# Row maxima of masked scores: key columns taken 512 and 256 at a time instead of 384 and 384

## The chip, the cores and the metric

The kernel runs on one core of a Trainium2 chip. The metric is the device time of one execution in microseconds (us). Before the change it is 643.86 us, the median of three runs (643.77 to 643.98).

## The reference

Two stages follow each other. The first is attention within clusters, for 4 batches of 8 heads, 768 tokens and 64 values per head:

```
q_assign = argmax over 16 centroids of cosine(q, centroid);  k_assign likewise
scores   = q k^T / sqrt(64), set to -1e9 where q_assign != k_assign
attn     = exp(scores - max(scores)) / (sum + 1e-9);   out = attn v
```

The second treats the 3072 rows of 512 values as tokens: a token is computed if its product with `w_skip` is positive, a gate of 8 experts picks one for it, and `relu(x w1) w2`, times the gate, is added to its row.

## The kernel before

Heads are worked on in pairs, i = 0 to 15; half a of a pair is one head. For a pair the kernel does the following.

**Operands.** q and k are split into a rounded part and a rest (`split_hi`, `split_lo`), the cluster of each token is found on VectorE (`assign`, `first_max`), and one-hot rows of the clusters are set under q and k (`masks`), so that one product of 96 rows gives the rounded score plus the mask.

**Maxima (`smax`, lines 577 to 587).** A product of 128 queries (tile j of 6) with 384 keys (half hf of 2) goes to a PSUM tile of 128x384, and VectorE reduces it to one column of `M`. For 6 tiles, 2 heads and 2 halves these are 24 products (line 582) and 24 reductions (line 584) a pair, 384 of each in all. `mneg` (line 598) then takes the larger of a tile's entries, and `mrows` (line 606) turns them and puts them as six more rows under q, so that a score product has the maximum subtracted.

**Scores (`score`).** For each of 24 (half, key tile, head) two products of 384 columns accumulate in one bank (lines 631, 632), ScalarE takes the exponential (line 634), and GpSimd adds up the sums (lines 640, 646). `avs` (line 657) multiplies the exponentials with v in groups of 12 records, into a bank of its own.

**Order.** Nothing is scheduled at run time. `steps` and `tasks` give every task a due time in steps (one score is one step, 24 to a pair; the numbers are in `PLAN` and, for the first pairs, in `FIRST`), and tasks are written out in that order; each engine then works its own queue in order. Maxima of pair i are due about 21 steps ahead of its first score, one a step, in two series of 12 with a small gap; so PE gets maxima of one pair between the scores of another. The routing of tokens to experts (`route_c`, `route_d` with line 996, and others) is put in between at the end of every fourth pair.

**Banks.** Eight PSUM banks of 128x512 stand as tiles. Bank 7 is kept for `avs` and for filler products; the other seven go round in a queue: `take` gives out the bank that was returned longest ago, and `give`, written right after the instruction that reads the bank, returns it. So with these calls the eighth tile uses the bank of the first, and PE waits at it until the reader of the first is done:

```
b = self.held[key] = self.free.popleft()
self.free.append(self.held.pop(key))
```

**Lead-in.** For pair 0 all of this has to happen before the first score. After each of the first 12 maxima products a filler product of 384 columns is written (`keep_busy`, line 280, `WARM`).

After the pairs come the experts (`experts`): products of 256 columns (`ph`) and 512 columns (`py`) in lines 1056 to 1058, with weights split by ScalarE and VectorE, rows gathered and scattered by indirect DMA.

Of the kernel before, what the change touches and what calls it, by code (L numbers as in the profile page):

```python
# [19 lines left out]
ALU = mybir.AluOpType  # L20
AX = mybir.AxisListType
PSUM = bass.MemoryType.PSUM

P = 128
H, S, D, NCL = 8, 768, 64, 16
HP = H // 2
HALF = S // 2
NB = HALF // P
KT = S // P
# [12 lines left out]
OT = 32  # L42
OC = P // OT
RING = 8
WARM = (0, 12, 3)


PLAN = {
# [33 lines left out]
class Kernel:  # L82
# [243 lines left out]
    def tasks(self, i):  # L326

        p, last = {**PLAN, **FIRST.get(i, {})}, i == self.npair - 1
        r = [(s, lambda s=s: self.score(i, s)) for s in range(NS)]
        add = lambda t, f, *a: r.append((t, lambda: f(i, *a)))  # L330
        if i:
            add(p["load"], self.load)
        add(p["load_v"], self.load_v)
        if i == 2:
            for a in range(2):
                add(8.0 + 6.0 * a - i * NS, self.set_rows, a)
        add(p["sims"], self.sims)
        add(p["assign"][0], self.assign, *p["assign"][1:])
        if i:
            for t in range(2):  # L340
                add(p["hi"][t], self.split_hi, t)
                add(p["lo"][t], self.split_lo, t)
            add(p["copies"][0], self.copies_hi)
            for t in range(2):
                add(p["copies"][1 + t], self.copies_lo, t)
            add(p["masks"][0], self.masks, *p["masks"][1:])
        else:
            for n in range(4):
                add(p["hi"][n], self.hi_first, n % 2, n // 2)
                add(p["lo"][n], self.lo_first, n % 2, n // 2)  # L350
            add(p["masks"], self.masks_first)
        t0, dt, gap, dt2 = (*p["smax"], p["smax"][1])[:4]
        for n in range(24):
            add(t0 + dt * n if n < 12 else t0 + 12 * dt + gap + dt2 * (n - 12), self.smax, n)
        for hf in range(2):
            add(p["mneg"][hf], self.mneg, hf)
            add(p["mrows"][hf][0], self.mrows, hf, *p["mrows"][hf][1:])
            for g in range(0, KT, GROUP):
                add(12 * hf + 2 * (g + GROUP) + p["av"], self.avs, hf, range(g, g + GROUP))
        if not last:  # L360
            add(p["sums"], self.sums, (0, 1))
            add(p["recip"], self.recip)
            for hf in range(2):
                add(p["xout"][2 if hf and i == self.npair - 2 else hf], self.xout, hf)
        if i == self.npair - HP - 1:
            for t, f in zip(p["early"], (self.early_lists, self.early_rows)):
                add(t, f)
        if last:
            for t, f, *a in self.ending(i):
                add(t, f, *a)  # L370
        elif i % HP == HP - 1:
            add(p["route"][0], self.route_a, i // HP)
            add(p["route"][1], self.route_gates, i // HP)
            add(p["route"][2], self.route_slots, i // HP)
        return r
# [199 lines left out]
                self.give((t, hf))  # L575

    def smax(self, i, n):
        c, nc = self.st[i], self.nc
        a, j, hf = n // KT % 2, n // (2 * KT) * NB + n // 2 % NB, n % 2
        c["m"] = self.M[i % 2]  # L580
        sm = self.take("sm", [P, HALF])
        nc.tensor.matmul(sm, lhsT=c["qm"][a][0:96, j * P:(j + 1) * P],  # L582
                         rhs=c["kb"][a][0:96, hf * HALF:(hf + 1) * HALF], start=True, stop=True)
        nc.vector.tensor_reduce(out=c["m"][:, j, a, hf:hf + 1], in_=sm, axis=AX.X, op=ALU.max)  # L584
        self.give("sm")
        if i == 0 and n in range(*WARM[:2]):
            self.keep_busy(1, WARM[2])

# [935 lines left out]
```

## Time and profile before

| | |
|---|---|
| runs | 643.77, 643.86, 643.98 us |
| profiled execution | 643.63 us; span 641.9 us from its first to its last instruction |
| VectorE (DVE) | 506.0 us busy (79%), 1047 instructions |
| ScalarE (ACT) | 425.9 us busy (66%) |
| GpSimd (POOL) | 364.0 us busy (57%) |
| line 584, reductions | 384 instructions |
| line 582, maxima products | 384 instructions, 356 ns each as recorded |

The profile is of one execution. PE is TensorE's products, PEld its weight loads. A product's record lasts longer than its share of the engine, since the next starts while it drains: what a product costs is the distance from its start to the next start. In a timeline the columns are start, duration (of a merged row: from first start to last end), engine, line, operation, tiles, shapes and count, and in brackets the idle time before with what ended it.

### The profile page before, as it was taken

How to read it: one execution, taken by the hardware profiler on the slowest of the kernel's cores; microseconds unless marked ns; L12 is line 12 of the kernel's file. 1: busy time of each engine (PE TensorE's matmuls, PEld its weight loads, DVE VectorE, ACT ScalarE, POOL GpSimd, SP SyncE). 2: the span in 40 equal slices, each digit the busy share in tenths (PEclk: the TensorE clock that was granted, in tenths of full speed). 3: DMA queues.
4: the chain of work that ended last, by engine and by line, in shares of the span. 5: the costliest groups of instructions: out<-in, count | busy, mean ns of one | idle time of the engine just before them, and what ended most of it. 6: DMA issues, size and time to landing. Idle time of an engine off the chain costs nothing.

```text
span 641.9 us, 12202 instructions
## 1 busy us (share of the span) xinstructions
PE 621.7 (97%) x3873; PEld 459.2 (72%) x3873; DVE 506.0 (79%) x1047; ACT 425.9 (66%) x963; POOL 364.0 (57%) x384
## 2 busy tenths in 40 slices
PE   7899999999999999999999999999999999999994
PEld 3566776676667766666767676646799899899793
DVE  6898787699998869999879997885889765855721
ACT  7377788788778877877878878833644644645510
POOL 8697887867867967778777778522043212121101
PEclk9999999999999999999999999999999999999998
DMA  7397748866786466555754652332395766765610
GB/s 215 92 228 204 189 125 210 228 205 176 206 231 179 129 172 168 170 140 162 206 151 124 174 135 75 99 117 86 117 312 196 255 222 223 240 206 177 240 44 36
DMA packets 54322, 110.10 MB, mean 172 GB/s; under 512 B 8599, under 2 KB 22807, under 8 KB 54256
## 3 DMA queue, kind: packets, MB, share of 16 engines
q1 hardware_dynamic: 51232, 101.92, 54.7%
q0 software_dynamic: 2624, 7.18, 3.3%
q8 instruction: 32, 0.52, 0.3%
q14 instruction: 34, 0.28, 0.2%
q10 hardware_dynamic: 400, 0.20, 0.1%
HBM read 60.93 MB, written 10.55 MB: 111 GB/s over the span
## 4 chain that ended last, share of the span: by engine, by line
PE 72%; DMA 10%; issue 9%; DVE 7%; ACT 1%; POOL 0%; POOLq 0%; DVEq 0%; ACTq 0%
PE ps L657 20%; PE ps L631 11%; PE ps L582 11%; PE ps L632 10%; DMA out<-yo,idw 7%; DMA xg<-out,idr 2%; PE ps L488 2%; DVE M L584 2%; PE ph L1058 2%; PE ph L1057 2%; PE ph L1056 2%; PE ps L693 2%; PE ps L756 2%; PE py L1057 1%; PE py L1056 1%
## 5 line engine op out<-in xcount | busy, mean ns | idle before, releaser
L646 POOL TENSOR_TENSOR acc<-acc,PT 128x384 f32<-128x384 f32 x246 | 244.0, 1020 | 42.2 <-ACT PT L634 41.9
L634 ACT ACTIVATE PT<-ps 128x384 f32<-128x384 f32 x384 | 183.2, 492 | 74.2 <-PE ps L632 62.1
L584 DVE TENSOR_REDUCE M<-ps 128x1 f32<-128x384 f32 x384 | 198.5, 550 | 40.3 <-PE ps L582 40.0
L657 PE MATMUL ps<-PT,vt 128*64 128x385 f32 x768 | 138.4, 495 | 0.1
L631 PE MATMUL ps<-D 102*128 102x384 f32 x384 | 134.9, 351 | 2.3 <-DVE M L584 1.7
L582 PE MATMUL ps<-D 96*128 96x384 f32 x384 | 134.4, 356 | 1.0 <-ACT D L562 1.0
L632 PE MATMUL ps<-D 128*128 128x384 f32 x384 | 130.0, 339 | 0.0
L657 PEld LDWEIGHTS ps<-PT,vt 128*64 128x64 f32 x768 | 49.3, 136 | 59.9 <-issue 55.3
L631 PEld LDWEIGHTS ps<-D 102*128 102x128 f32 x384 | 72.8, 190 | 23.8 <-issue 18.6
L582 PEld LDWEIGHTS ps<-D 96*128 96x128 f32 x384 | 73.5, 192 | 21.0 <-issue 14.4
L640 POOL TENSOR_TENSOR acc<-PT 128x384 f32<-128x384 f32 x64 | 54.5, 870 | 58.4 <-ACT PT L634 37.1
L1214 POOL DMA_INDIRECT out<-yo,idw x15 | 20.0, 1335 | 112.6 <-DVE yo L1090 95.3
L632 PEld LDWEIGHTS ps<-D 128*128 128x128 f32 x384 | 73.0, 190 | 0.0
L1342 ACT ACTIVATE hh<-ph 128x256 fp32r<-128x256 f32 x56 | 21.4, 383 | 46.4 <-PE ph L1058 46.4
L1343 DVE SCALAR_TENSOR_TENSOR hl<-ph,hh 128x256 fp32r<-128x256 f32 x56 | 23.6, 422 | 33.6 <-ACT hh L1342 33.6
L1314 ACT ACTIVATE D<-wraw 128x1024 fp32r<-128x1024 f32 (+1 forms) x45 | 44.2, 1002 | 6.5 <-PE py L1058 4.7
L1056 PE MATMUL ph<-x2l,D 128*128 128x256 f32 x168 | 47.7, 284 | 0.0
L1057 PE MATMUL ph<-x2h,D 128*128 128x256 f32 x168 | 47.5, 283 | 0.0
L1056 PE MATMUL py<-D,hh 128*128 128x512 f32 x112 | 45.0, 402 | 0.0
L1315 DVE TENSOR_TENSOR D<-wraw,D 128x1024 fp32r<-128x1024 f32 (+1 forms) x29 | 34.3, 1183 | 6.3 <-ACT D L1314 5.6
L778 ACT ACTIVATE x<-ps,rs 128x64 f32<-128x64 f32 x162 | 36.1, 322 | 3.5 <-issue 1.2
L439 DVE TENSOR_TENSOR raw<-raw,D 128x768 fp32r<-128x768 f32 x28 | 38.2, 1363 | 0.0
(314 smaller groups left out, 1050.5 us busy)
## 6 DMA issues: line engine op xcount, KB each, us to landing
wraw<-w SPq DMA_DIRECT2D x72, 512.0 KB, 4.7
D<-D SPq DMA_DIRECT2D x124, 192.0 KB, 3.4
raw<-qk SPq DMA_DIRECT2D x16, 768.0 KB, 5.5
D<-raw SPq DMA_DIRECT2D x60, 192.0 KB, 4.2
vt<-v SPq DMA_DIRECT2D x16, 384.0 KB, 4.6
out<-x SPq DMA_DIRECT2D x31, 192.0 KB, 3.6
D<-mk SPq DMA_DIRECT2D x120, 24.0 KB, 2.0
out<-yo,idw POOLq DMA_INDIRECT x15, 4.3
```

Of the source, the lines that this page charges most:

```text
L439: eng.tensor_tensor(out=lo.bitcast(F32R), in0=lo, in1=c[f"hi{t}"].bitcast(F32), op=ALU.subtract)
L582: nc.tensor.matmul(sm, lhsT=c["qm"][a][0:96, j * P:(j + 1) * P], rhs=c["kb"][a][0:96, hf * HALF:(hf + 1) * HALF], start=True, stop=True)
L584: nc.vector.tensor_reduce(out=c["m"][:, j, a, hf:hf + 1], in_=sm, axis=AX.X, op=ALU.max)
L631: nc.tensor.matmul(ps, lhsT=c["kb"][a][:MR, ks], rhs=c["qm"][a][:MR, sl], start=True, stop=False)
L632: nc.tensor.matmul(ps, lhsT=c["kc"][a][:, ks], rhs=c["qc"][a][:, sl], start=False, stop=True)
L634: nc.scalar.activation(out=pt, in_=ps, func=AF.Exp, scale=D ** -0.5)
L640: nc.gpsimd.tensor_tensor(out=acc, in0=self.pt(i, s - 2)[:, :HALF], in1=pt, op=ALU.add)
L646: (nc.vector if dve else nc.gpsimd).tensor_tensor(out=acc, in0=acc, in1=pt, op=ALU.add)
L657: nc.tensor.matmul(av[a * D:(a + 1) * D, :], lhsT=c["vt"][:, kt, a * D:(a + 1) * D], rhs=self.pt(i, hf * 2 * KT + kt * 2 + a), start=(kt = ...
L1056: mm(ps, lhsT=ah, rhs=bl, start=first, stop=False)
L1057: mm(ps, lhsT=ah, rhs=bh, start=False, stop=False)
L1314: nc.scalar.activation(out=h[:, cs], in_=r[:, cs], func=AF.Copy)
```

## The change

Four 384-column products of two neighbouring (head, query tile) units become four products into three banks: 512 keys of the first unit, then 256 keys of the first and 256 of the second side by side, then 512 keys of the second. Each bank has one reduction; the middle one reduces 128x2x256 to two columns. A pair has 18 calls in place of 24, due every 4/3 of the former distance. The units of a half are (head 0: tiles 0, 1), (head 0 tile 2, head 1 tile 2), (head 1: tiles 0, 1). In the lead-in 9 filler products of 512 columns replace 12 of 384.

```
-WARM = (0, 12, 3)
+WARM = (0, 9, 4)
...
-        for n in range(24):
-            add(t0 + dt * n if n < 12 else t0 + 12 * dt + gap + dt2 * (n - 12), self.smax, n)
+        for n in range(18):
+            add(t0 + dt * n * 4 / 3 if n < 9 else t0 + 12 * dt + gap + dt2 * (n - 9) * 4 / 3, self.smax, n)
...
-        a, j, hf = n // KT % 2, n // (2 * KT) * NB + n // 2 % NB, n % 2
         c["m"] = self.M[i % 2]
-        sm = self.take("sm", [P, HALF])
-        nc.tensor.matmul(sm, lhsT=c["qm"][a][0:96, j * P:(j + 1) * P],
-                         rhs=c["kb"][a][0:96, hf * HALF:(hf + 1) * HALF], start=True, stop=True)
-        nc.vector.tensor_reduce(out=c["m"][:, j, a, hf:hf + 1], in_=sm, axis=AX.X, op=ALU.max)
+        m = c["m"].rearrange("p j a h -> p (j a h)")
+        j0, (two, part) = n // 9 * NB, divmod(n % 9, 3)
+        ends = (((0, 0), (0, 1)), ((0, 2), (1, 2)), ((1, 0), (1, 1)))[two]
+        at = [((j0 + j) * 2 + a) * 3 for a, j in ends]
+        sm = self.take("sm", [P, 512])
+        parts = ((0, 0, 512),) if part == 0 else ((1, 256, S),) if part == 2 else ((0, 512, S), (1, 0, 256))
+        n0 = 0
+        for u, k0, k1 in parts:
+            a, j = ends[u]
+            nc.tensor.matmul(sm[:, n0:n0 + k1 - k0], lhsT=c["qm"][a][0:96, (j0 + j) * P:(j0 + j + 1) * P],
+                             rhs=c["kb"][a][0:96, k0:k1], start=True, stop=True)
+            n0 += k1 - k0
+        if part == 1:
+            out, sm = m[:, at[0] + 1:at[1] + 1:at[1] - at[0] - 1], sm.rearrange("p (u k) -> p u k", u=2)
+        else:
+            out = m[:, at[0]:at[0] + 1] if part == 0 else m[:, at[1] + 1:at[1] + 2]
+        nc.vector.tensor_reduce(out=out, in_=sm, axis=AX.X, op=ALU.max)
         self.give("sm")
```

## Rows read from the trace of the kernel before

**Rows 1.** Page, busy time: engine, busy us, share of the span, instructions.

```profile
PE 621.7 (97%) x3873; PEld 459.2 (72%) x3873; DVE 506.0 (79%) x1047; ACT 425.9 (66%) x963; POOL 364.0 (57%) x384
```

**Rows 2.** Stretches: from:to, length; busy us of PE, PEld, DVE, ACT, POOL; clock, DMA.

```profile
175.00:189.00 14.00, 12.97 (x88) 8.74 (x86) 13.62 (x30) 10.01 (x29) 9.59 (x11) 1.00 0.84 213
189.00:250.00 61.00, 61.00 (x370) 42.37 (x371) 50.91 (x100) 48.89 (x120) 45.88 (x48) 1.00 0.61 168
```

**Rows 3.** Waits of PE: who waited for whom, us in total, times, longest.

```profile
PE ps L996 <- DVE M L584: 2.1, 2, 1.0
PE ps L631 <- DVE M L584: 1.7, 2, 0.9
```

**Rows 4.** Timeline of PE, 384-column products following each other, first and last.

```profile
36.93 0.34 PE L582 MATMUL ps<-D 96*128 96x384 f32 x1
...
39.58 0.34 PE L582 MATMUL ps<-D 96*128 96x384 f32 x1
```

**Rows 5.** Timeline of PE in the experts, 256-column products and the first of 512.

```profile
519.78 0.28 PE L1057 MATMUL ph<-x2h,D 128*128 128x256 f32 x1
...
523.25 0.40 PE L1056 MATMUL py<-D,hh 128*128 128x512 f32 x1
```

**Rows 6.** Timeline of PE in the experts, 512-column products, first and last.

```profile
477.66 0.39 PE L1056 MATMUL py<-D,hh 128*128 128x512 f32 x1
...
480.84 0.39 PE L1058 MATMUL py<-vtW,hl 128*128 128x512 f32 x1
```

**Rows 7.** Groups of VectorE by form: busy us, mean ns of one, idle before, releaser.

```profile
L584 DVE TENSOR_REDUCE M<-ps 128x1 f32<-128x384 f32 x384 | 198.5, 550 | 40.3 <-PE ps L582 40.0
...
L513 DVE TENSOR_REDUCE mwc<-eqc 128x24 f32<-128x384 f32 x16 | 8.8, 552 | 0.5
...
L1252 DVE TENSOR_REDUCE ot<-ob 128x8 f32<-128x768 f32 x1 | 0.9, 940 | 0.0
```

**Rows 8.** Timeline, second maxima of pair 0.

```profile
21.69 0.51 PE L582 MATMUL ps<-D 96*128 96x384 f32 x2
...
23.66 5.73 DVE L584 TENSOR_REDUCE M<-ps 128x1 f32<-128x384 f32 x12
...
24.24 0.44 PE L631 MATMUL ps<-D 102*128 102x384 f32 x1 [0.81 <-DVE M L584]
...
28.26 2.16 PE L657 MATMUL ps<-PT,vt 128*64 128x385 f32 x12
```

**Rows 9.** Timeline, maxima of pair 1 behind a stretch of VectorE work.

```profile
42.18 0.42 PE L582 MATMUL ps<-D 96*128 96x384 f32 x1
...
43.85 0.33 PE L582 MATMUL ps<-D 96*128 96x384 f32 x1
...
44.51 2.84 DVE L584 TENSOR_REDUCE M<-ps 128x1 f32<-128x384 f32 x6
...
45.09 0.45 PE L631 MATMUL ps<-D 102*128 102x384 f32 x1 [0.90 <-DVE M L584]
```

**Rows 10.** Timeline of PE at the routing, first of two such places.

```profile
184.06 0.44 PE L582 MATMUL ps<-D 96*128 96x384 f32 x1
...
185.76 0.33 PE L582 MATMUL ps<-D 96*128 96x384 f32 x1
187.13 0.38 PE L996 MATMUL ps<-rhs,oht 128*128 128x80 bf16 x6 [1.03 <-DVE M L584]
187.33 0.42 PE L631 MATMUL ps<-D 102*128 102x384 f32 x1
```

**Rows 11.** Timeline of VectorE, the same place.

```profile
186.55 1.91 DVE L584 TENSOR_REDUCE M<-ps 128x1 f32<-128x384 f32 x4
```

**Rows 12.** Timeline, first maxima of pair 0.

```profile
12.92 0.84 ACT L564 ACTIVATE D<-ps 32x384 fp32r<-32x384 f32 x2
...
13.07 0.45 PE L582 MATMUL ps<-D 96*128 96x384 f32 x1 [0.66 <-ACT D L562]
...
13.55 5.86 DVE L584 TENSOR_REDUCE M<-ps 128x1 f32<-128x384 f32 x12
```

**Rows 13.** Timeline of weight loads in the experts, one of those between 256-column products.

```profile
520.02 0.19 PEld L1057 LDWEIGHTS ph<-x2h,rawW 128*128 128x128 f32 x1
```

## The prediction

> **What bounds the kernel now.** I read the busy times first: PE has 97% of the span [rows 1]. A busy PE need not be a full one, so the second view is the stretches: in 61 us of ordinary attention PE is busy for all 61.00 us while VectorE has 50.91 [rows 2]; in the 14 us around the routing it is VectorE that is nearly full (13.62) and PE that has a hole (12.97). The third view, PE's waits, says where VectorE holds PE up: line 996 twice for 2.1 us in all, line 631 twice for 1.7 us, both for a reduction of line 584 [rows 3]. The fourth is the distance of products in a timeline. From 36.93 to 39.58 lie 15 distances, so a 384-column product costs 0.177 us, with no gap between maxima and scores [rows 4]. The kernel is therefore bound by PE's stream, except for the lead-in and a few places at which PE waits for a bank that a late reduction holds. A cheaper VectorE is worth something only there.
>
> **PE's columns.** Four products stay four, 1536 columns stay 1536, so everything hangs on how the cost of a product goes with its width. In the experts 29 distances of 256 columns take 523.25 - 519.78 = 3.47 us, 0.120 us each [rows 5], and 14 of 512 columns take 480.84 - 477.66 = 3.18 us, 0.227 us each [rows 6]. So 0.227 + 0.120 = 0.347 against 2 x 0.177 = 0.354: 7 ns less per unit of one query tile and head, and with 192 units (6 tiles, 2 heads, 16 pairs) 1.3 us less. Per product 0.120 and 0.227 leave 13 to 14 ns over the columns at 2.4 GHz (106.7 and 213.3 ns), and the 384-column one 17 ns over 160. No attention row has the new widths: the extra 3 ns may belong to the place (other traffic) and not to the width. Then 512 and 256 cost 0.230 and 0.123 and nothing is gained. I take the middle, -0.65 us, and keep 0 and -1.3.
>
> The Trainium skill (page "TensorE: Matmul & The Clock Gate", section "Back-to-back issue gap") gives a distance of N/2.4 + 2.5 ns at the full clock. By it 512 and 256 columns come to 216 and 109 ns and two of 384 to 325 as well, so this term would be 0. The rows are 11 to 15 ns above the rule at every width; it agrees in that a product has the same extra at any width, which speaks against the 1.3 us.
>
> **VectorE.** 384 reductions become 288. One of 384 columns lasts 0.550 us, one of 768 columns 0.940, so 512 columns should last 0.550 + 128 x (0.390/384) = 0.680; a reduction into 24 groups lasts 0.552, so the two groups of the middle bank cost nothing extra [rows 7]. Back to back, 12 take 5.73 us, (5.73 - 0.55)/11 = 0.47 apart [rows 8]; 512 columns should be 0.60 apart. In all 384 x 0.47 - 288 x 0.60 = 7.7 us less of VectorE. This lies beside PE's stream: VectorE already idles 40 us in front of these reductions because it waits for PE [rows 7]. I count nothing for it by itself; if a pair were bound by VectorE, it would be up to 0.5 us a pair.
>
> **The bank waits.** A bank comes round after seven takes. What matters is how much work PE can do in seven takes before it meets the bank of a maximum whose reduction is late. Before, maxima and scores alternate: four maxima and three scores are 4 x 0.177 + 3 x 0.354 = 1.77 us. After, there are three maxima calls to four scores, a call costs 0.236 on average, so seven takes are 3 x 0.236 + 4 x 0.354 = 2.12 us: 0.35 us more. The reduction that is waited for lasts 0.13 us longer. So a wait should shrink by 0.22 us, and by up to one score (0.354) more or less, as the new due times put the first maximum later or earlier against VectorE's other work. Place by place:
>
> Second maxima of pair 0. PE sends the first two at 21.69, VectorE begins the twelve only at 23.66 and PE gets on at 24.24; the wait is 0.81 us, and by 28.26 all twelve are through [rows 8]. Here VectorE is the bound: 5.73 us become 0.68 + 8 x 0.60 = 5.48, -0.25 us. Bounds 0 and -0.8; I take -0.3.
>
> Pair 1. The maximum of 42.18 is reduced from 44.51 on, behind pair 2's assignment; PE ends its products begun at 43.85 and stands until 45.09, 0.90 us of idle record [rows 9]. By the due times (-16.3 and 0.95 x 4/3) the first maximum here moves from step 19.95 to 20.27, behind score 20: +0.22 and about a score, less a longer VectorE queue. Bounds +0.1 and -0.9; I take -0.45.
>
> The routing, twice. The product of line 996 takes the bank of the maximum of 184.06, seven takes before, which is reduced from 186.55 [rows 10, 11]. By the new due times maxima are due at 8.23, 9.57 and 10.9 where 7.9, 8.9, 9.9 and 10.9 stood; line 996 is due right behind 10.9, so it is then the sixth take behind the late maximum, not the seventh. It goes through with score 11, and score 12 waits instead. That is one score (0.354) and 0.19 us more of seven takes, less 0.13 for the longer reduction and 0.1 for the two wider ones in VectorE's queue ahead: -0.3, and 0.05 for columns done earlier. Bounds 0 and -1.0 each; I take -0.35 each.
>
> **The lead-in.** The first product now needs keys 0 to 511, that is also the second key half's mask rows, the first of the two copies that begin at 12.92 and end 0.84 later, so about 13.34; the first product began at 13.07 [rows 12]. It starts some 0.3 us later and takes 0.05 longer, and the twelve reductions (5.86 us, 0.48 apart) become 0.68 + 8 x 0.61 = 5.58. Sum +0.35 - 0.28, about +0.1 us; bounds -0.3 and +0.4. Fillers are 9 x 512 for 12 x 384 columns, the same 4608. The same dependence exists for all pairs, but their mask rows are due 13 steps ahead of the maxima (5 for pair 1), so it is hidden; uncovered it would be one copy a pair.
>
> **Moved steps.** The last call of a series is due a third of a step earlier than before, so `mneg` and `mrows` have no less time. The blocks of other products (line 657, 488, 693) keep their neighbours. No DMA is issued or moved by this change.
>
> **Sum.** -0.3 - 0.45 - 0.7 + 0.1 - 0.65 = -2.0 us. The experts run behind attention with PE in its stream, so the gain should pass through. The profiled execution has 643.63 us (641.9 of span and 1.7 around it), 0.23 below the median; on the median I forecast 641.9.
>
> **Rivals.**
>
> Hidden after all. VectorE's order, not the banks, sets when PE gets on: the longer reductions give back what the seven takes win, and the columns cost the same. Left are -0.3 and -0.25 in pair 0 and 1 and +0.1 in the lead-in: 643.4. For it: at the routing VectorE is full [rows 2]. Against: PE is in front of the bank each time, and the seven takes do grow.
>
> More. The columns cost what the experts' rows say (-1.3) and the waits shrink to half of 3.8 us [rows 3]: -1.9 and +0.1, 640.8; with less in the lead-in 640.5.
>
> Slower. A weight load is recorded with 0.19 us [rows 13], and 256 columns give it only 107 ns of cover. If in attention a product cannot end before the next one's load, 256 columns keep the distance of 384: 192 x (0.177 - 0.120) = 10.9 us, 653. Break-even is a distance of 0.354 - 0.227 + 1.35/192 = 0.134 us. Against: the experts hold 0.120 with the same loads [rows 5, 13]. The same page of the Trainium skill (section "LDWEIGHTS (loading the stationary operand)") has P/1.2, 107 ns for 128 columns as an estimate: just as long as the columns, without reserve.
>
> Clock. PE ends the lead-in's products earlier against VectorE's end, and stands longer before the first score. No stretch here is below 1.00 [rows 2]; if the clock fell to half for some 3 us, about +1.5 on top, 645.4 with nothing gained.
>
> **How the numbers follow.** Forecast 0.50, its own range 640.7 to 643.0; hidden 0.27; more 0.11; slower 0.08; clock 0.04. About 0.2% (1.3 us, 642.6 to 645.1) is what a measurement of this kernel can tell from no change. Of the forecast 0.05 lies inside: faster 0.45 + 0.11 = 0.56, same 0.05 + 0.26 = 0.31, slower 0.13. Below 640.4 I leave 0.07, above 644.4 0.12.
>
> **What would show it.** 288 reductions of about 0.68 us; distances of 0.227 (or 0.230) behind 512 columns and 0.120 (or 0.123) behind 256; line 996 no longer waiting for line 584; the wait of 45.09 shorter; the first score of pair 0 within 0.4 us of where it was. Wrong would be a distance of 0.135 or more behind 256 columns, new waits for line 584 in ordinary pairs, or a clock below 1.00.

## The result: slower, 647.8 us against 643.7

The changed kernel takes 647.81 us (median of six runs, 646.61 to 648.07), the kernel before, beside it on the same chip, 643.7 (643.61 to 643.98). The ratio is 1.0058 [1.0045, 1.0071]: 0.6% slower, where 641.9 was forecast and 644.4 was the upper end. The profiled execution has 648.07 us, its span is 646.3. Two executions that were longer as a whole (one of the kernel before with 691 us, one of a later kernel with 1543) are left out of all counts, ranges and medians below.

The page of the changed kernel, busy times and clock in slices, answers to [rows 1]:

```profile
PE 624.8 (97%) x3870; PEld 453.0 (70%) x3870; DVE 491.3 (76%) x951; ACT 418.1 (65%) x963; POOL 358.7 (56%) x384
PEclk9799999999999999999999999999999999999998
```

VectorE is busy 14.7 us less, 11.2 of it in the reductions (198.5 us before, 187.3 after, where records that overlap count once), and PE 3.1 us longer: the work that was taken away lay beside the path, as said. The second slice of the clock shows a 7, so the next view is the stretches. First the changed kernel (columns as in [rows 2]), then the one stretch of the kernel before that is compared and not among those rows:

```profile
19.80:26.70 6.90, 6.33 (x21) 5.64 (x22) 6.31 (x11) 3.71 (x8) 2.64 (x3) 0.51 0.16 60
...
150.00:175.00 25.00, 24.16 (x150) 15.75 (x149) 23.28 (x47) 18.68 (x50) 17.70 (x19) 1.00 0.70 190
175.00:189.00 14.00, 13.79 (x91) 8.71 (x90) 13.05 (x27) 10.99 (x32) 9.60 (x11) 1.00 0.76 195
```

```profile
150.00:175.00 25.00, 25.00 (x156) 17.31 (x154) 23.53 (x54) 20.38 (x53) 19.24 (x21) 1.00 0.72 192
```

Two new things: 6.9 us at a granted clock of 0.51 (the 1.2 GHz level) in the lead-in, and a hole of 0.84 us in PE between 150 and 175, where there was none. The 0.21 us of hole left between 175 and 189 are not all of the one at the routing: in the changed kernel it lies across 189 us and is 0.59 us long (the wait before 189.38, shown below), where [rows 2] have 1.03. PE's waits of the changed kernel (us, times, longest) name the second one:

```profile
PE ps L590 <- DVE M L597: 2.5, 3, 0.8
...
PE ps L644 <- DVE M L597: 1.2, 2, 0.6
```

Lines 590 and 597 are the maxima product and its reduction (582 and 584 before), 644 and 645 the scores (631, 632), 619 and 670 are 606 and 657. The waits of [rows 3] are gone: line 996 (now 1009) doesn't wait at all. In their place stand two of 0.6 us at the scores, and three of 0.8 us at a maxima product, which no row of before has.

**Where the time went.** The start of the first product group of line 657 (670) marks each pair. Its difference to the kernel before, in the two profiled executions:

| at the start of pair | changed minus before, us |
|---|---|
| 0 (28.26 before) | +1.50 |
| 1 | +0.35 |
| 2 | +0.64 |
| 5 | +0.90 |
| 6 | +2.03 |
| 7 | +1.80 |
| 9 | +1.98 |
| 10 | +3.08 |
| 11 | +2.83 |
| 13 | +3.01 |
| 14 | +4.15 |
| end of the span | +4.38 |

So: +1.5 with the clock at half; about -1.15 behind pair 0; +1.1 three times (on the way to pairs 6, 10 and 14); -0.25 behind the first two of these, where the routing now waits less; and 0.08 to 0.09 in each ordinary pair.

**The three steps of 1.1 us.** Here the timeline of the changed kernel has to be read on three engines at once. These are rows picked from all three, in order of start, with the idle record in brackets:

```profile
155.37 0.54 DVE L521 STREAM_TRANSPOSE ss<-ps 128x384 f32<-128x384 f32 x1
156.40 0.69 DVE L597 TENSOR_REDUCE M<-ps 128x1 f32<-128x512 f32 x1 [0.49 <-PE ps L590]
157.01 0.54 DVE L502 TENSOR_REDUCE mxc<-ss 128x24 f32<-128x384 f32 x1
...
166.28 0.94 DVE L439 TENSOR_TENSOR raw<-raw,D 128x768 fp32r<-128x768 f32 x1
167.09 1.68 POOL L653 TENSOR_TENSOR acc<-PT 128x384 f32<-128x384 f32 x2 [1.95 <-ACT PT L647]
167.15 0.84 DVE L955 CAST vals<-g 128x6 bf16<-128x6 f32 x1
168.02 0.77 DVE L958 TENSOR_TENSOR g<-g,vals 128x6 f32<-128x6 f32 x1
168.27 0.34 PE L645 MATMUL ps<-D 128*128 128x384 f32 x1
168.72 0.68 DVE L597 TENSOR_REDUCE M<-ps 128x1 f32<-128x512 f32 x1
169.45 0.50 PE L590 MATMUL ps<-D 96*128 96x512 f32 x1 [0.84 <-DVE M L597]
```

The same instructions in the kernel before (L942 and L945 are 955 and 958, L640 is 653):

```profile
154.50 0.56 DVE L521 STREAM_TRANSPOSE ss<-ps 128x384 f32<-128x384 f32 x1
155.10 0.55 DVE L502 TENSOR_REDUCE mxc<-ss 128x24 f32<-128x384 f32 x1
...
164.16 0.94 DVE L439 TENSOR_TENSOR raw<-raw,D 128x768 fp32r<-128x768 f32 x1
165.02 0.16 DVE L942 CAST vals<-g 128x6 bf16<-128x6 f32 x1
165.22 0.17 DVE L945 TENSOR_TENSOR g<-g,vals 128x6 f32<-128x6 f32 x1
...
166.20 1.68 POOL L640 TENSOR_TENSOR acc<-PT 128x384 f32<-128x384 f32 x2 [1.96 <-ACT PT L634]
```

At 154 the changed kernel is 0.87 us behind, on VectorE as on PE (+0.90 at pair 5, which begins at 157). Then VectorE meets a reduction between two steps of the assignment, and stands 0.49 us until PE has written its bank: by the due times a maximum now falls on step 5.57 (-18.43), and the assignment's transposition is due at 5.55, its next step at 5.62. Line 502 is 1.91 us behind, line 439 2.12. VectorE is busy 23.28 of these 25 us, so nothing is caught up. The two small steps of the gate that follow come late enough to run beside GpSimd's additions and last 0.84 and 0.77 us instead of 0.16 and 0.17 (more on this in the last section). Behind them is the reduction whose bank PE takes seventh from there: PE stands from 168.27 to 169.45, 1.18 us from product to product where 0.18 is usual.

**The ordinary pairs.** Between the turning of the maxima and the product group of line 670 the changed kernel is 0.08 us slower. First the changed kernel, then the one before:

```profile
116.90 0.58 ACT L697 ACTIVATE oT<-ps,vm 128x384 f32<-128x384 f32 x1
117.21 0.27 PE L619 MATMUL ps<-ident,MX 128*128 128x128 f32 x1
117.53 0.20 PEld L670 LDWEIGHTS ps<-PT,vt 128*64 128x64 f32 x4 [0.35 <-ACT oT L697]
```

```profile
116.25 0.58 ACT L684 ACTIVATE oT<-ps,vm 128x384 f32<-128x384 f32 x1
116.64 0.27 PE L606 MATMUL ps<-ident,MX 128*128 128x128 f32 x1
116.88 0.20 PEld L657 LDWEIGHTS ps<-PT,vt 128*64 128x64 f32 x4 [0.27 <-ACT oT L684]
```

The group writes bank 7, and ScalarE's copy of the last contents (line 697) ends 0.05 us before the group's weights are loaded, in both. But the turning (line 619) begins 0.31 us after the copy does instead of 0.39; in the new order no maxima product stands directly ahead of it. PE waits out the difference: 0.32 us from turning to group, 0.24 before.

### The profile page after: what moved, and what is told of

Read it like the earlier page. It is cut to its first block, busy times and chain, and to the rows that moved or that the text cites. A ratio compares the mean times of both kernels' runs of the same rounds, so it can differ in the third digit from the quotient of the medians.

```text
span 646.3 us, 12145 instructions
## 1 busy us (share of the span) xinstructions
PE 624.8 (97%) x3870; PEld 453.0 (70%) x3870; DVE 491.3 (76%) x951; ACT 418.1 (65%) x963; POOL 358.7 (56%) x384
## 4 chain that ended last, share of the span: by engine, by line
PE 79%; issue 7%; DMA 6%; ACT 3%; POOL 2%; DVE 2%; POOLq 0%; ACTq 0%; DVEq 0%
PE ps L670 21%; PE ps L644 11%; PE ps L590 10%; PE ps L645 10%; DMA out<-yo,idw 3%; PE ph L1071 3%; PE ph L1070 3%; PE ph L1069 3%; PE py L1070 2%; PE py L1069 2%; PE py L1071 2%; PE ps L488 2%; ACT PT L647 2%; PE ps L769 2%; PE ps L706 2%
## 5 line engine op out<-in xcount | busy, mean ns | idle before, releaser
L659 POOL TENSOR_TENSOR acc<-acc,PT 128x384 f32<-128x384 f32 x246 | 239.9, 1003 | 48.0 <-ACT PT L647 47.7
L597 DVE TENSOR_REDUCE M<-ps 128x1 f32<-128x512 f32 (+1 forms) x288 | 187.3, 683 | 61.7 <-PE ps L590 61.0
L647 ACT ACTIVATE PT<-ps 128x384 f32<-128x384 f32 x384 | 176.2, 492 | 83.4 <-PE ps L645 68.7
L644 PE MATMUL ps<-D 102*128 102x384 f32 x384 | 137.5, 358 | 1.8 <-DVE M L597 1.2
L645 PE MATMUL ps<-D 128*128 128x384 f32 x384 | 131.4, 342 | 0.0
L590 PE MATMUL ps<-D 96*128 96x512 f32 (+1 forms) x384 | 119.5, 356 | 3.6 <-DVE M L597 2.5
L630 ACT ACTIVATE D<-ps,blocks 6x256 fp32r<-6x256 f32 x84 | 33.3, 457 | 1.7 <-PE ps L619 1.0
```

The costliest lines, as they stand in the source:

```text
L590: nc.tensor.matmul(sm[:, n0:n0 + k1 - k0], lhsT=c["qm"][a][0:96, (j0 + j) * P:(j0 + j + 1) * P], rhs=c["kb"][a][0:96, k0:k1], start=True, ...
L597: nc.vector.tensor_reduce(out=out, in_=sm, axis=AX.X, op=ALU.max)
L644: nc.tensor.matmul(ps, lhsT=c["kb"][a][:MR, ks], rhs=c["qm"][a][:MR, sl], start=True, stop=False)
L645: nc.tensor.matmul(ps, lhsT=c["kc"][a][:, ks], rhs=c["qc"][a][:, sl], start=False, stop=True)
L647: nc.scalar.activation(out=pt, in_=ps, func=AF.Exp, scale=D ** -0.5)
L659: (nc.vector if dve else nc.gpsimd).tensor_tensor(out=acc, in0=acc, in1=pt, op=ALU.add)
```

## The experiments

Each kernel was run beside the kernel before on the same chip, whose median is 643.7 to 643.9 throughout. Of the granted clock each run has only its mean over the span; where in the span it was lost can be read in the profiled executions alone. There a mean of 0.996 or 0.997 goes with full clock but for the last few us of the span, 0.992 to 0.995 with 3.4 us at half clock in or just behind the lead-in, and 0.991 with 6.8 us. The other runs are sorted by these means; "the clock intact" means 0.992 or more, short dips included.

**One step of VectorE's order.** The assignment's transposition and the two steps behind it are put 0.1 step earlier (due at 5.45, 5.52 and 5.54), the rest stays: the maximum of 5.57 no longer falls between. PE's order is the same instruction for instruction.

```
-"assign": (-42.45, 0.07, 0.02, 2.0, 0.02, 0.02)
+"assign": (-42.55, 0.07, 0.02, 2.1, 0.02, 0.02)
```

> The changed kernel; in ordinary pairs the assignment's transposition and its first two steps are due 0.1 step earlier, so that VectorE has them ahead of the maximum due at step 5.57, as it had before the change. PE's order is the same. Theory 1 (VectorE's order): in the changed kernel the reduction of that maximum stands between the transposition and the next step, waits for a product that PE sends late, and delays the assignment by about 1 us; at the three routing places (168, 272, 375 us) this runs into GpSimd's additions and PE then waits about 1.0 us for a bank. Then the three waits go: 3.1 us less than the changed kernel, 644.7 with the clock fallen in the lead-in, 643.5 without. Rival (the wider reductions themselves lengthen VectorE's queue at the routing): 647.8 as the changed kernel, the three waits stay.

Measured: 644.17 us (643.40 to 645.29, 12 runs), ratio 1.0003 [0.9995, 1.0012]. Its timeline:

```profile
155.09 0.54 DVE L521 STREAM_TRANSPOSE ss<-ps 128x384 f32<-128x384 f32 x1
155.66 0.55 DVE L502 TENSOR_REDUCE mxc<-ss 128x24 f32<-128x384 f32 x1
...
166.72 0.17 DVE L955 CAST vals<-g 128x6 bf16<-128x6 f32 x1
166.92 0.77 DVE L958 TENSOR_TENSOR g<-g,vals 128x6 f32<-128x6 f32 x1
167.62 0.68 DVE L597 TENSOR_REDUCE M<-ps 128x1 f32<-128x512 f32 x1
...
167.99 0.34 PE L645 MATMUL ps<-D 128*128 128x384 f32 x1
168.35 0.50 PE L590 MATMUL ps<-D 96*128 96x512 f32 x1
```

Line 502 follows line 521 directly, line 955 is back at 0.17 us, and PE's stop is 0.36 us instead of 1.18. With the clock intact the median is 644.1 (10 runs), that of the changed kernel 646.6 (2 runs): 2.5 us of the loss hang on one place of VectorE's queue. The three waits were expected to go altogether; about 0.3 us of each is left.

**Three more fillers in the lead-in.** Behind the last of the first nine maxima four filler products are written instead of one.

```
-            self.keep_busy(1, WARM[2])
+            self.keep_busy(4 if n == WARM[1] - 1 else 1, WARM[2])
```

> The changed kernel with three more filler products of 512 columns behind the last product of the lead-in, which change nothing else. Theory 1: the clock falls because PE stands for 2.25 us ahead of 19.8 us instead of 1.75; with the fillers the granted clock stays at 1.00 and the time is that of the changed kernel's undisturbed-clock runs, about 646.6 (1.2 us less than 647.8). Rival: the clock falls for what PE did earlier in the lead-in, and stays fallen: 647.8.

Measured: 646.62 us (645.82 to 647.26, 5 runs), 1.0036 [1.0023, 1.0049]; the lowest clock of the five is 0.992. So 1.2 us of the loss are the clock's, and about 2.9 are not. That the clock would stay at 1.00 throughout did not come true: in the profiled execution it was at half for 3.4 us from 13.9 us on, ahead of the place at which PE stands.

**Both.** 

> Both edits: assignment ahead of the maximum, and three more fillers. If both causes are right and add up: 647.8 - 3.1 - 1.2 = 643.5, the kernel before within 0.1%. If the clock's loss is caught up at the waits behind it: 644.5. Rival (wider reductions): 646.6.

Measured: 643.91 us (643.46 to 644.77, 11 runs), 1.0000 [0.9991, 1.0008]. The two causes add up, and with both mended the rest of the change is worth nothing. In its trace pair 0 is 0.28 us ahead of the kernel before and pair 1 1.43; at the end of attention 0.17 are left. The stops at the three places are still there with 0.36 us each, and the ordinary pairs take 26.09 and 25.45 us against 26.00 and 25.36.

**The kernel before with a like swap built in.** 384-column maxima as before; the assignment's next step is put 0.3 later, so that here too a reduction comes between. PE's order is unchanged.

```
-"assign": (-42.45, 0.07, 0.02, 2.0, 0.02, 0.02)
+"assign": (-42.45, 0.37, 0.02, 1.7, 0.02, 0.02)
```

> The kernel before, with 384-column maxima as they were; only the two steps behind the assignment's transposition are due 0.3 step later in ordinary pairs, so that one maximum's reduction stands between them in VectorE's queue as in the changed kernel. PE's order is the same. Theory 1: waits of line 582 for line 584 appear at the routing and cost up to 1 us at three places: 645 to 647. Rival (the wider reductions): 643.7, no new wait.

Measured: 646.88 us (646.75 to 648.57, 5 runs), 1.0042 [1.0029, 1.0055]. So it takes no wide product to lose 3 us, a swap in VectorE's queue does it. But the size was expected for another reason: no wait of line 582 appeared at the routing. The loss lies at scores of ordinary pairs that wait for line 584 (at 86.64 us, for one, 0.49 us from product to product instead of 0.18), which take up to 0.4 us more a pair. The profiled execution is the one of 648.57 us, with 6.8 us at half clock behind the lead-in.

**The second series later.** On top of both mendings the last nine maxima of a pair get due times 0.9 step later, to put them behind the gate's steps.

```
-"smax": (-21.1, 1.0, -0.4)
+"smax": (-21.1, 1.0, 0.5)
```

> Assignment ahead of the maximum, three more fillers (both as in e3_both), and the second series of maxima of ordinary pairs 0.9 step later, so that a maximum is due at 19.4, ahead of the turned maxima (19.5), as a maxima product was there in the kernel before, and none between 13.57 and 15.4. Theory 1 (what is left of the loss is again the order of queues): the 0.09 us that each ordinary pair still loses lies at line 670 behind line 619, where PE waits for ScalarE's copy of bank 7; with 0.24 us more of PE's work ahead of it that goes (about -0.8), and the 0.3 us at the three routing places goes too, since no maximum is queued behind the split and the gate steps (-0.9): 642.2. Rival (the loss lies in the wider products or reductions): 643.9 as e3_both.

Measured: 645.65 us (645.08 to 646.05, 8 runs), 1.0029 [1.0019, 1.004]. I had expected a gain, and the three stops came back with 1.18 to 1.21 us, though the assignment is not interrupted here.

```profile
165.75 0.83 DVE L955 CAST vals<-g 128x6 bf16<-128x6 f32 x1
166.62 0.77 DVE L958 TENSOR_TENSOR g<-g,vals 128x6 f32<-128x6 f32 x1
167.32 0.16 DVE L611 TENSOR_REDUCE MX<-M 128x6 f32<-128x18 f32 x1
167.40 1.87 DVE L597 TENSOR_REDUCE M<-ps 128x1 f32<-128x512 f32 x3
...
168.13 0.50 PE L590 MATMUL ps<-D 96*128 96x512 f32 x1 [0.84 <-DVE M L597]
```

The interrupted assignment is thus one way into the stop, not its only cause. What both have in common stands ahead of the reduction that PE needs: the gate's two steps at 0.8 us each.

**The gate's steps behind the reduction.** The changed kernel as it is, interrupted assignment and lead-in included; only the gate's line 955 and 958 move behind the one reduction that is waited for.

```
-61.67, 61.68, 67.67, 67.68
+62.6, 62.61, 67.67, 67.68
```

> The changed kernel; two small gate steps of the routing on VectorE (lines 955 and 958) are due 0.9 step later, behind the reduction of the maximum due at 14.5 in place of ahead of it, at three places; PE's order is the same, the assignment stays as changed. Theory 1 (the wait of about 1.0 us is the sum of what stands ahead of that one reduction, late VectorE plus split plus the two steps that last 0.8 each while GpSimd adds): without the two steps ahead of it the reduction ends 1.6 us sooner and the three waits go: 3 us less than the changed kernel, 644.8 with the clock fallen, 643.6 without. Rival (VectorE is late enough to hold the bank without these steps): 647.8 or 646.6 as before.

Measured: 645.86 us (644.13 to 647.13, 11 runs), 1.0026 [1.0016, 1.0036]. The runs fall into two groups by the clock: five with 0.992 to 0.996 take 644.13 to 644.60 us, six with 0.989 and 0.990 take 645.86 to 647.13. The first group (median 644.2) stands against 646.6 for the changed kernel with its clock intact: 2.4 us less, where 3 were expected. The stops of 1.18 us at the maxima product are gone, but at each of the three places a stop of 0.67 us has come at line 619, and PE still falls back by 0.5 us there instead of 1.1. By the traces 1.8 us of the gain lie at these places. So the two steps ahead of the reduction make about half of each 1.1 us. With the assignment moved instead, 0.3 us of each is left: the two edits act on the same wait, this one takes 0.6 us of it, that one 0.8.

**The whole grid later.** Instead of the assignment the maxima's due times, their grid, are shifted: the first series by 0.15 step, the second by 0.9. The fillers stay in.

```
-"smax": (-21.1, 1.0, -0.4)
+"smax": (-20.95, 1.0, 0.35)
```

> The changed kernel with three more fillers; the assignment as changed, but all maxima of ordinary pairs due 0.15 step later and the second series 0.75 more, so that the maximum of 5.57 falls behind the assignment's first steps (5.72) and that of 13.57 behind line 670 and the split (13.72). Theory 1: both queue effects go by the other side; the three routing waits are absent, 642 to 643. Rival (wider products or reductions): 646.6 as with the fillers alone.

Measured: 643.26 us (642.88 to 643.70, 11 runs), 0.9994 [0.9985, 1.0003], with one new stop of 1.19 us in the last pair: there a reduction stands behind 1.22 and 0.87 us of VectorE's work for the experts.

**The last pair as it was.** `FIRST` also gives pair 15 its old due times.

```
+    15: {"smax": (-21.1, 1.0, -0.4)},
```

> e7_whole_later with the last pair's maxima at the due times of the changed kernel (there a maximum stood behind the expert weights' split, 1.2 us, and the route's sums, and PE waited 1.0 us at 396.5 us). Theory 1: that wait goes, 1.0 us less: 642.3, faster than the kernel before by 0.2%. If the wait only moves, 643.3.

Measured: 642.42 us (642.01 to 644.02, 11 runs), 0.9983 [0.9973, 0.9992]: 0.8 us less, about what the stop had. No trace of this kernel is read.

**The copy of bank 7 earlier.** On top of that ScalarE's first copy is due 0.2 step earlier; its order alone changes.

```
-"oT": (3.5, 3.55)
+"oT": (3.3, 3.55)
```

> e8_last_pair with ScalarE's copy of bank 7 (the first half's result of line 670) due 0.2 step earlier, ahead of one exponential instead of behind it; PE's order is the same. Theory 1: the 0.07 us that ordinary pairs still lose against the kernel before is PE waiting for that copy at line 670 behind line 619 (0.299 us there for 0.241 before). Then ordinary pairs take 26.0 and 25.36 us again and the time falls by 0.5 to 0.9 us: 641.6. Rival (it is the wider products themselves): as e8, and the distance behind line 619 shortens while another lengthens.

Measured: 640.80 us (640.13 to 641.53, 5 runs), 0.9951 [0.9937, 0.9965]: 2.9 us below the kernel before, and 1.6 below the last version, about twice what was expected. In its trace (the execution of 641.53 us) (line 671 is 670) the group follows the turning after 0.21 us and no longer waits for the copy:

```profile
115.48 0.27 PE L620 MATMUL ps<-ident,MX 128*128 128x128 f32 x1
115.69 0.20 PEld L671 LDWEIGHTS ps<-PT,vt 128*64 128x64 f32 x4 [0.29 <-ACT PT L648]
```

Ordinary pairs take 25.97 and 25.32 us instead of 26.09 and 25.45. Against the kernel before, pair 2 begins 0.96 us earlier, the two routing places bring 0.44 us each, and an ordinary pair brings 0.03 to 0.04. The gate's steps are at 164.83 and 165.03 with 0.17 us each, and there is no stop at the three places.

**Fewer fillers in the kernel before.** Nine fillers of 384 columns instead of twelve: PE ends its lead-in's products earlier and stands longer, 2.28 us from start to start instead of 1.75. Nothing else changes.

```
-WARM = (0, 12, 3)
+WARM = (0, 9, 3)
```

> The kernel before without the last three of its twelve filler products in the lead-in, so that PE stands for about 0.5 us longer ahead of 19.7 us, as in the changed kernel. If that is what makes the clock fall in some runs (4 of 6 of the changed kernel, none of 6 of the kernel before), a good part of the runs here are 1 to 1.8 us longer than 643.8, up to 645.5. If not, 643.7 with the spread of the kernel before.

Measured: 643.91 us (643.45 to 645.84, 11 runs), 1.0009 [0.9998, 1.002]. Four of the eleven have a clock of 0.990 or 0.991 and take 645.15 to 645.84 us, the other seven take 643.45 to 644.03.

**The copy earlier in the kernel before, and then all due times.** Two controls: are the edits of the last version worth the same without the wide products?

```
-"oT": (3.5, 3.55)
+"oT": (3.3, 3.55)
```

> The kernel before with only ScalarE's copy of bank 7 due 0.2 step earlier (the edit of e9_bank7_copy). If that edit alone brought what e9 has over the kernel before (2.9 us), 641 to 642. Theory 1: before, PE waits there 0.241 us at line 657 behind line 606, some 0.04 to 0.09 us of it for the copy, so 13 ordinary pairs gain 0.5 to 1.2 us: 642.5 to 643.2, and the wider products without their queue waits bring the rest.

Measured: 643.48 us (642.91 to 644.11, 11 runs), 0.9993 [0.9984, 1.0002], where the kernel before has 643.86. Its ordinary pairs take 25.97 and 25.33 us, as with the wide products above: there the width is worth nothing.

The second has the shifted grid, the last pair's old one and the copy, on 384-column maxima, with the lead-in of the kernel before:

> The kernel before, 384-column products and reductions as they were, with all due times of e9_bank7_copy (maxima 0.15 step later, second series 0.75 more, last pair as it was, copy earlier). If the due times alone bring e9's gain, 641. Theory 1: the one-a-step series keeps the waits of line 996 and of pairs 0 and 1, and gains the copy alone: 642.5 to 643.5, or more if a new wait comes.

Measured: 647.08 us (646.60 to 647.16, 5 runs), 1.0045 [1.0031, 1.0059], with a wait for a reduction that [rows 3] has twice now five times (line 632 is 631):

```profile
PE ps L632 <- DVE M L585: 3.5, 5, 1.1
```

This control shows the stop of the changed kernel without a wide product. At three of the five places the gate's two steps (lines 943 and 946 here) stand ahead of the reduction: at 167.73 and 270.94 us PE stands 0.6 us from start to start, behind steps of 0.16 and 0.71 us; at 374.89 us it stands 1.41, behind steps of 0.84 and 0.77.

The gain of 2.9 us belongs to neither part: the copy alone brings about 0.4, not clear of noise, and these due times with 384 columns cost 3.2. It is the wide products with a grid of their own. Whether some other grid would help the 384-column kernel was not tried.

## Why the prediction was wrong

**The step that failed** is the one on the bank waits, with the sentences on moved steps. It looked at the four waits that the trace had, and asked how each would shrink; it checked of the moved calls that `mneg` keeps its time and that other products keep their neighbours. VectorE's order was not gone through, and neither was what stands ahead of the turning (line 606), which lost its maxima product. But a reduction is written at the due time of its product, in a queue that is worked in order, and with a spacing of 4/3 nearly every one falls between other instructions than before. One such place made three new waits, together +3.4 us (three steps of 1.1), and the copy of bank 7 another 0.08 to 0.09 in each of seven ordinary pairs, +0.6. Both stood at nothing in the sum. "New waits for line 584 in ordinary pairs" stood in the list of what would prove the prediction wrong; they came, at the pairs with the gate's steps, but their price was never worked out, and the rival on the slower side was another one. Shown by runs: moving the start of the assignment alone gives most of it back (2.5 us), moving the gate's steps alone about as much (2.4, of which the traces put 1.8 at the three places), and a like stop appears in the kernel before when its due times are shifted.

**The columns** were sized at -0.65 us, with 0 as a bound. It is 0. In the changed kernel:

```profile
174.12 0.40 PE L590 MATMUL ps<-D 96*128 96x512 f32 x1
174.35 0.34 PE L644 MATMUL ps<-D 102*128 102x384 f32 x1
...
174.71 0.40 PE L590 MATMUL ps<-D 96*128 96x256 f32 x2
174.94 0.34 PE L644 MATMUL ps<-D 102*128 102x384 f32 x1
```

In the median over many such calls, the start of the next product lies 0.233 us behind 512 columns (0.227 in the experts, [rows 6]) and 0.24 behind the pair of 256 together with 0.006 that the second score behind it takes longer: 0.233 + 0.240 + 0.233 = 0.706 us for two units, against 4 x 0.177 = 0.708. The bound that said "the place, not the width" was right. The slower rival with 256 columns at the distance of 384 is refuted by the same rows. The rival "hidden after all" had the columns right, and missed the waits as the forecast did.

**VectorE.** The sizes were right: 192 reductions to one column last 684 ns and 96 to two columns 681, for 680 worked out. So was that a cheaper VectorE is worth nothing by itself.

```profile
L597 DVE TENSOR_REDUCE M<-ps 128x1 f32<-128x512 f32 x192 | 127.6, 684 | 46.3 <-PE ps L590 45.7
L597 DVE TENSOR_REDUCE M<-ps 128x2 f32<-128x512 f32 x96 | 65.3, 681 | 15.4 <-PE ps L590 15.4
```

**The waits that were priced** went the way they were to go. Lead-in and second maxima of pair 0 were +0.1 and -0.3; with the clock intact (both mendings) the sum at pair 0 is -0.28. Pair 1 was -0.45 and brought -1.15, of which 0.3 were lost again by pair 2. Line 996 passes and score 12 waits instead, as described:

```profile
187.97 0.39 PE L1009 MATMUL ps<-rhs,oht 128*128 128x80 bf16 x6
...
188.45 0.34 PE L645 MATMUL ps<-D 128*128 128x384 f32 x1
189.38 0.44 PE L644 MATMUL ps<-D 102*128 102x384 f32 x1 [0.59 <-DVE M L597]
```

The two places gave -0.23 and -0.25 for -0.35 forecast. Taken by themselves these terms are about -1.6 us (-0.28 - 0.85 - 0.5), close to the -1.35 that they were given. They are what the last version keeps, with -0.96 by pair 2 and twice -0.44 at the routing.

**The clock** was a rival at a chance of 0.04, +1.5 us. It came, in four of the six runs (clock 0.991), and cost 1.2: 647.76 to 648.07 against 646.61 and 646.66. (By the traces it is 1.8 at pair 0: +1.50 here, -0.28 in the gate-steps kernel, which has the same lead-in and kept its clock.) The mechanism named, a longer standstill ahead of the first score, agrees with the counts. The last filler begins at 17.51 us and the next product at 19.76:

```profile
17.51 0.39 PE L280 MATMUL ps<-ones_bf 128*128 128x512 bf16 x1
19.76 0.46 PE L619 MATMUL ps<-ident,MX 128*128 128x128 f32 x1 [1.85 <-DVE MX L611]
```

That is 2.25 us from start to start; it was 1.75 (17.99 to 19.74) in the kernel before. Counted over all kernels, a clock of 0.991 or less occurred in 12 of 29 runs with the changed lead-in (the changed kernel 4, the first experiment 2, the gate's steps 6) and in none of 51 with the three extra fillers. In the kernel before it occurred in 3 of 82 runs, and with three fillers less in 4 of 11. What the two lead-ins in which it is frequent share is the standstill, 2.25 and 2.28 us; their filler columns are 4608, as many as in the kernel before, and 3456.

**What stays open.** Why the stops came back in full with the later second series is read from its trace, and not tried by itself: there the gate's steps are slow, and the reduction that PE waits for stands behind them. The long dip in the kernel before (3 of the 82 runs beside the experiments) is too rare to say what sets it off there, and the standstill does not explain the short dips: in the traces of the first two experiments they end before it begins (14.07 to 17.49 and 13.93 to 17.34 us). That GpSimd's additions are what slows the gate's steps is read from the traces; no run moved the additions alone.

## What to carry to other kernels

When a change spaces out calls anew, go through the queue of the engine that serves them, instruction by instruction at one place of each kind, and look for every spot where it now waits for something between two steps of other work; the waits that the old trace has are only those that can shrink. A change of tile sizes and the due times it needs are one change: here the sizes cost 2.9 us (4.1 with the clock's part) with the due times that came with them and gain 2.9 with others and an earlier copy, which cost the old sizes 3.2. Check what a cheaper warm-up leaves idle, even if it does the same number of columns.

## What the runs showed of the hardware

Small VectorE instructions on SBUF can last as long as a GpSimd instruction beside them. In the changed kernel lines 955 and 958 (128x6) end at 167.99 and 168.79 us, and GpSimd's two additions at 167.09, 0.84 us each by 1.68 for two, at about 167.93 and 168.77; where GpSimd is idle, in the kernel before, they last 0.16 and 0.17 us (at 165.02 and 165.22), and in the same kernel 0.84 and 0.92 at 170.40 and 171.27, beside a row of additions. The Trainium skill (page "SBUF — State Buffer", section "Who interferes with whom") says that VectorE and GpSimd share one pair of SBUF ports, given out as an exclusive lock, and that on trn2 a `tensor_reduce` never contends for it. The trace agrees in both: the small instructions end with GpSimd's, and a reduction of 128x48 at 154.80 in the changed kernel lasts 0.19 us in the middle of an addition (154.34 to 155.20).

The mean granted clock differs between runs of one and the same kernel: from 0.991 to 0.997 in the kernel before, from 0.989 to 0.996 in the one with the gate's steps moved. The traces show what lies behind such means: no dip, 3.4 us or 6.8 us at half clock in or behind the lead-in. The short dip can't be told from none in the time (the kernel before with 0.992 and 0.993: 643.5 to 644.4 us, with 0.996 and 0.997: 643.3 to 644.1, but for one run of 644.97), the long one costs 1.1 to 1.8 us of 644.
